# x and w_in converted to bf16 by the loads themselves: an induced-attention and PReLU feed-forward kernel on one core

## The chip, the core and the metric

The kernel runs on one core of a Trainium2 chip. The metric is the device time of one execution in microseconds. The engines are called as in the profile: PE (matrix products; PEld is its weight load), DVE, ACT and POOL (elementwise work), SP (here only an issuer of transfers). A name with q (SPq, POOLq) is the engine's instruction queue, which is worked through in order. 16 DMA engines carry the transfers that any queue issues.

## The reference

Four batches of 12,480 rows with 128 channels, 32 inducing rows, and a hidden layer of 2,048:

```
def mab(q, kv):
    s = scale * (q @ kv.transpose(0, 2, 1))
    s = s - s.max(-1, keepdims=True)
    a = np.exp(s)
    a /= a.sum(-1, keepdims=True) + 1e-09
    return a @ kv
h = mab(I, x)                      # 32 rows attend to all rows of a batch
y = mab(x, h).reshape(49920, 128)  # every row attends to those 32
t = y @ w_in
out = (np.maximum(t, 0.0) + alpha * np.minimum(t, 0.0)) @ w_out
```

All inputs and the output are f32 in memory.

## The kernel before

**Pieces.** Each batch of x is cut into six full pieces of 2,048 rows (1 MB, 16 tiles of 128 rows) and one of 192 rows (`xs_left`, `xn_left`). The order of work on them is the list `pieces`: the first full piece, the short one, then the other five. Within a full piece partition p holds 16 consecutive rows, so a load reads 8 KB in a row per partition.

**First stage, per batch.** `a_load` (L244) loads a piece as f32 into one of four `xs` buffers, from SP's queue. `a_cast` (L260) makes it bf16 (`xn`), on POOL (L272, L277), once on ACT (L270). It is then transposed to `xT`: by PE in the first batch (`a_turn_pe`, L286, copies on DVE L296 and ACT L294), by a transposing transfer from SP's queue in the others (`a_turn`, L281). `a_scores` (L310, L328, L337) gives the scores against the inducing rows with a running extremum, `a_exp` (L350) the exponentials, `a_fac` (L368, L375) the rescaling of earlier pieces, `a_e1` or `a_e1_pe` (L397, L398) a transpose of these, and `a_h` (L410, L423) adds the piece to h, for which it needs `xn` again. The end of the stage (`a_max`, `a_factors`, `a_den`, `a_sum`) gives `hT` (L478), and `a_w` (L486) the product `HW` of h with w_in (`w_in_b`, bf16).

**Second stage and main loop.** For each group of 2,048 rows DVE, ACT and POOL make the 32 softmax weights of each row (`b_scores` to `b_mul`; on POOL: L605, the sums L591 and L615, and L636), which a transposing transfer turns (`b_turn`, L645) into `a`. The main loop has 392 visits, four for each block of four tiles. A visit makes four products `hh` from `a` and `HW` (L692), applies a ReLU to them on ACT (L704) or DVE (L706), and the next visit multiplies these with `W1` (L717), which is w_out times one minus alpha. The rest of the PReLU is linear and enters through `Amat` (`linear`, L742). `finish` (L753) copies the sums (L768, L770) and SP stores them, from three `ob` buffers.

**What orders the work.** The first batch's first stage, the head, has nothing beside it: it is written out by hand as a string of steps, `order` (L911), where c is a cast, t a PE transpose, s scores, x exponentials, e their transpose, h the sum, w some products that keep PE busy. Ahead of it the first five pieces are loaded (L800); `load_next` (L851) issues the sixth and seventh, then w_in and w_out, as casts of earlier pieces free a buffer. `prepare_weights` (L901), behind step h3, casts w_in on POOL (L902), turns it (L903) and makes `W1` (L877) and `AW` (L886) on POOL. The first stage of the other batches is spread over the main loop: `at(n, ...)` puts a step behind visit n. A planner (`Plan`) gives each ReLU and copy to ACT or DVE from costs listed with these steps; loads, casts and POOL's steps carry no cost. In it the load of a piece stands three visits ahead of the number m of its piece, the cast six behind, the transpose eight behind, the scores fifteen behind. `tails` (L543) loads, casts and turns the short pieces of all batches for the last two blocks.

Of the kernel before, what the change touches and what calls it, by code (L numbers as in the profile page):

```python
# [22 lines left out]
P = 128  # L23
R = 4
ST = 16
# [6 lines left out]
def kernel(  # L32
# [9 lines left out]
    nc = tc.nc  # L42
    f32 = mybir.dt.float32
    bf16 = mybir.dt.bfloat16

    B, N, C = x.shape
# [25 lines left out]
    place = {s: p for p, s in enumerate(pieces)}  # L72

    const = ctx.enter_context(tc.tile_pool(name="const", bufs=1))
    xs_pool = ctx.enter_context(tc.tile_pool(name="xs", bufs=4))
    xn_pool = ctx.enter_context(tc.tile_pool(name="xn", bufs=sum(full)))
    xt_pool = ctx.enter_context(tc.tile_pool(name="xt", bufs=2))
    s1_pool = ctx.enter_context(tc.tile_pool(name="s1", bufs=3))
    e1_pool = ctx.enter_context(tc.tile_pool(name="e1", bufs=6))
# [147 lines left out]
    def new_state(b):  # L227
        st = State()
        st.b = b
        st.xT = xt_pool.tile([C, NT, P], bf16, name="xT", tag="xT")  # L230
        st.xn, st.xs, st.s1, st.e1T, st.e1 = {}, {}, {}, {}, {}
        st.e2, st.m2, st.den2, st.rc, st.rep = {}, {}, {}, {}, {}

        st.mx = sm_pool.tile([P, NS], f32, name="mx", tag="mx")
        st.rm = sm_pool.tile([P, NS], f32, name="rm", tag="rm")
        st.fac = sm_pool.tile([P, NS], f32, name="fac", tag="fac")
        st.da = sm_pool.tile([P, NS], f32, name="da", tag="da")
        st.den = sm_pool.tile([P, NS], f32, name="den", tag="den")
        st.hs = h_pool.tile([P, C], f32, name="hs", tag="hs")
        nc.gpsimd.memset(st.mx[:], HIGH)  # L240
        nc.gpsimd.memset(st.da[:], 0.0)
        return st

    def a_load(st, s):  # L244
        r0, nt, last = supers[s]
        if full[s]:
            st.xs[s] = xs_pool.tile([P, ST, C], f32, name="xs", tag="xs")
            nc.sync.dma_start(
                out=st.xs[s][:],
                in_=x[st.b, r0 : r0 + nt * P, :].rearrange("(p j) c -> p j c", p=P),  # L250
            )
        else:
            st.xs[s] = xs_left
            for t in range(nt):
                n = last if t == nt - 1 else P
                nc.sync.dma_start(
                    out=xs_left[:n, t, :], in_=x[st.b, r0 + t * P : r0 + t * P + n, :]
                )

    def a_cast(st, s, part=None, act=False):  # L260

        r0, nt, last = supers[s]
        xs = st.xs[s]
        if full[s]:
            if s not in st.xn:
                st.xn[s] = xn_pool.tile([P, ST, C], bf16, name="xn", tag="xn")
            h = ST // 2
            ts = slice(0, ST) if part is None else slice(part * h, part * h + h)
            if act:
                nc.scalar.copy(out=st.xn[s][:, ts], in_=xs[:, ts])  # L270
            else:
                nc.gpsimd.tensor_copy(out=st.xn[s][:, ts], in_=xs[:, ts])  # L272
        else:
            st.xn[s] = xn_left
            for t in range(nt):
                n = last if t == nt - 1 else P
                nc.gpsimd.tensor_copy(out=xn_left[:n, t, :], in_=xs[:n, t, :])  # L277

    def a_turn(st, s):
        nt = supers[s][1]  # L280
# [262 lines left out]
    def tails(part):  # L543

        if part == 0:
            nc.sync.dma_start(out=xb[:, :B, :], in_=whole(x))
            for i, w in enumerate(halves):
                nc.sync.dma_start(out=xb[w, B:, :], in_=half(x, i))
        elif part == 1:
            nc.gpsimd.tensor_copy(out=xbn[:], in_=xb[:])  # L550
        else:
            nc.sync.dma_start_transpose(out=xbT[:], in_=xbn[:].rearrange("p j c -> p (j c)"))

# [229 lines left out]
        plan.then(work)  # L783


    ident32 = const.tile([P, P], f32, name="ident32")
    make_identity(nc, ident32[:])
    st = new_state(0)
    ind_f = const.tile([M, C], f32, name="ind_f")
    nc.scalar.dma_start(out=ind_f[:], in_=inducing)  # L790
    al_f = const.tile([NK, P], f32, name="al_f")
# [1 line left out]
    alT = const.tile([P, NK], f32, name="alT")  # L793
    hTs = [const.tile([C, M], bf16, name=f"hT{b}") for b in range(B)]
    HWs = [const.tile([P, NV * P], bf16, name=f"HW{b}") for b in range(B)]
    xb = const.tile([P, NB, C], f32, name="xb")
    xbn = const.tile([P, NB, C], bf16, name="xbn")
    xbT = const.tile([C, NB, P], bf16, name="xbT")
    xs_left = const.tile([P, supers[-1][1], C], f32, name="xs_left")
    for s in pieces[:5]:  # L800
        a_load(st, s)
    xn_left = const.tile([P, supers[-1][1], C], bf16, name="xn_left")
    e1T_left = const.tile([P, supers[-1][1] * P], bf16, name="e1T_left")
    for t in (xn_left, e1T_left):
        nc.vector.memset(t[:], 0.0)
    ident = const.tile([P, P], bf16, name="ident")
    nc.vector.tensor_copy(out=ident[:], in_=ident32[:])

# [21 lines left out]
    AW = rep_pool.tile([P, NK, C], bf16, name="AW")  # L830
    winT = rep_pool.tile([P, NK, C], bf16, name="winT")
    W1 = const.tile([P, NK, C], bf16, name="W1")
    w_in_b = const.tile([C, DFF], bf16, name="w_in_b")
    Amat = const.tile([C, C], bf16, name="Amat")
    ind_b = const.tile([M, C], bf16, name="ind_b")
    nc.scalar.copy(out=ind_b[:], in_=ind_f[:])
# [9 lines left out]
    )  # L846

    a2s = {}
    w_in_f = w_out_f = None

    def load_next(p):  # L851

        nonlocal w_in_f, w_out_f
        if p + 5 < NS:
            a_load(st, pieces[p + 5])
        elif w_in_f is None:
            w_in_f = xs_pool.tile([C, DFF], f32, name="w_in_f", tag="xs")
            nc.sync.dma_start(out=w_in_f[:], in_=moe_w_in)
        elif w_out_f is None:
            w_out_f = xs_pool.tile([P, NK, C], f32, name="w_out_f", tag="xs")  # L860
            nc.sync.dma_start(out=w_out_f[:], in_=moe_w_out.rearrange("(k p) c -> p k c", p=P))

    def warm(n):

        ps = sums(1)
# [33 lines left out]
        nc.vector.tensor_copy(out=Amat[:], in_=ps[:])  # L899

    def prepare_weights():  # L901
        nc.gpsimd.tensor_copy(out=w_in_b[:], in_=w_in_f[:])  # L902
        nc.sync.dma_start_transpose(out=winT[:], in_=w_in_b[:])  # L903
        for i in range(NV):
            weights(i, nc.gpsimd)
        for i in range(NV):
            linear_weights(i)
# [1 line left out]


    order = """  # L911
        c00 t00 c01 t02 t01 c10 c21 c20 t10 s0 x0 t22 s1 c31 x1 t21 t20 c30 t32 t31 s2 f1 e0 c41
        t30 e1 x2 c40 c51 f2 c50 t42 s3 e2 t41 x3 f3 c60 t40 t51 t52 c61 h0 s4 t50 e3 t60 x4 t62
        t61 s5 f4 e4 s6 h1 h2 x5 h3 m0 h4 x6 e5 r0 e6 w1 f5 h5 w1 f6 h6 w2 d0 w1 g0 w2
    """
    assert NS == 7 and len(pieces) == 7 and not full[-1]
    cast = set()
    for step in order.split():
        f, p, part = step[0], int(step[1]), int(step[2:] or 0)
        s = pieces[p]  # L920
        if f == "c":
            a_cast(st, s, part, act=(p == NS - 1 and part == 1))
            cast.add((p, part))
            if p != 1 and (p, 1 - part) in cast:
                load_next(p - (p > 1))
        elif f == "t":
            a_turn_pe(st, s, part)
        elif f == "w":
            warm(p)
        elif f in "mrdg":  # L930
            {"m": a_max, "r": a_factors, "d": a_den, "g": a_sum}[f](st)
        else:
            {"s": a_scores, "x": a_exp, "f": a_fac, "e": a_e1_pe, "h": a_h}[f](st, s)
        if step == "h3":
            prepare_weights()
# [74 lines left out]
    for b, s, nt in groups[1:]:  # L1010
# [13 lines left out]
        at(when[5], on, b, b_rec, s, nt, cost=[("v", 160)])  # L1024
        at(when[6], on, b, b_mul, s, nt)
        at(when[7], on, b, b_turn, s, 0, nt)
    for part in range(3):
        at(first[B, 0] - 50 + 8 * part, tails, part)
    for b in range(B - 1):
        n = first[b, 0] - 1  # L1030
        if b:
            at(n - 4, lambda b=b: states.__setitem__(b + 1, new_state(b + 1)))
        for p, s in enumerate(pieces):
            m = n + (8 * (p - 1) if p > 1 else p)
            f = full[s]
            if b or p > 1:
                at(m - 3, on, b + 1, a_load, s)
            at(m + 6, on, b + 1, a_cast, s)
            at(m + 8, on, b + 1, a_turn, s)
            at(m + 15, on, b + 1, a_scores, s, cost=[("s", 310), ("v", 800 if f else 460)])  # L1040
            at(m + 16, on, b + 1, a_exp, s, cost=[("a", 717 if f else 430)])
            at(m + 18, on, b + 1, a_fac, s, cost=[("a", 450)] if p else [])
            at(m + 17, on, b + 1, a_e1, s)
            at(m + (24 if f else 26), on, b + 1, a_h, s, cost=[("s", 320), ("v", 260)])
        m = n + 8 * (NS - 2) + 15
        at(m + 2, on, b + 1, a_max, cost=[("a", 200)])
        at(m + 4, on, b + 1, a_factors, cost=[("s", 800), ("v", 70), ("a", 205)])
        at(m + 8, on, b + 1, a_den, cost=[("s", 500), ("v", 370)])
        at(m + 11, on, b + 1, a_sum, cost=[("s", 500), ("v", 110)])
        at(m + 12, on, b + 1, a_w, cost=[("s", 310)])  # L1050
        at(m + 12, on, b + 1, a_w_copy, cost=[("a", 487)])
        at(m + 15, on, b + 1, a_lin, cost=[("s", 160), ("v", 190)])
# [66 lines left out]
```

## Time and profile before

| | us |
|---|---|
| median of three runs | 602.05 (601.94 to 602.33) |
| profiled execution, first to last instruction (span) | 600.4 |
| median less span | 1.65 |
| PE, ACT, DVE, POOL busy in the span | 585.3, 552.9, 520.5, 218.3 |
| casts of x on POOL, 29 full or half pieces | 45.1 |
| cast of w_in on POOL | 1.89 |
| bytes moved | 80.51 MB, 134 GB/s on average |

The profile gives no time of the profiled execution beside its span; the runs' times are without a profile. PE, DVE, ACT and POOL in the profile are shares of busy time. The views that the prediction uses are: the slices, in which a digit is the busy share of a fortieth of the span in tenths; the chain that ended last, which goes back from the last instruction to what released each step; the timeline, whose rows are start, length, engine, line, operation and shapes, with the idle time ahead and its releaser in brackets; the busy time by stages; and the DMA view, which gives GB/s in fortieths of the stretch asked for.

### The profile page before, as it was taken

How to read it: one execution, taken by the hardware profiler on the slowest of the kernel's cores; microseconds unless marked ns; L12 is line 12 of the kernel's file. 1: busy time of each engine (PE TensorE's matmuls, PEld its weight loads, DVE VectorE, ACT ScalarE, POOL GpSimd, SP SyncE). 2: the span in 40 equal slices, each digit the busy share in tenths (PEclk: the TensorE clock that was granted, in tenths of full speed). 3: DMA queues.
4: the chain of work that ended last, by engine and by line, in shares of the span. 5: the costliest groups of instructions: out<-in, count | busy, mean ns of one | idle time of the engine just before them, and what ended most of it. 6: DMA issues, size and time to landing. Idle time of an engine off the chain costs nothing.

```text
span 600.4 us, 22604 instructions
## 1 busy us (share of the span) xinstructions
PE 585.3 (97%) x9405; PEld 438.4 (73%) x9407; DVE 520.5 (87%) x935; ACT 552.9 (92%) x1130; POOL 218.3 (36%) x253
## 2 busy tenths in 40 slices
PE   5899999999999999999999999999999999999997
PEld 3567777777777777777777777777777777777775
DVE  4678988988998998988898988988899899899895
ACT  3889999999999999999989999999999999999995
POOL 5655625313415526223236255134034034044110
PEclk9999999999999999999999999999999999999999
DMA  8859979333176999542256998841431331531321
GB/s 338 277 156 209 210 182 213 88 83 73 55 207 163 232 204 202 113 81 72 64 140 189 238 226 158 161 84 53 79 83 55 89 84 43 117 97 46 86 68 46
DMA packets 122198, 80.51 MB, mean 134 GB/s; under 512 B 103744, under 2 KB 106096, under 8 KB 118896
## 3 DMA queue, kind: packets, MB, share of 16 engines
q1 hardware_dynamic: 122016, 79.05, 54.0%
q8 instruction: 73, 1.20, 0.8%
q14 instruction: 29, 0.24, 0.1%
q10 hardware_dynamic: 80, 0.02, 0.0%
HBM read 28.07 MB, written 25.56 MB: 89 GB/s over the span
## 4 chain that ended last, share of the span: by engine, by line
PE 94%; ACT 2%; DMA 1%; DVE 1%; SPq 0%; issue 0%; POOL 0%; DVEq 0%; ACTq 0%
PE bp L717 65%; PE hh L692 22%; PE bp L742 2%; PE hh L525 2%; DMA xs<-in_x_dram 1%; PE hh L410 1%; PE hh L310 1%; ACT e1T L350 0%; ACT e L398 0%; ACT den L375 0%; ACT xT L294 0%; PE hh L486 0%; ACT fac L368 0%; ACT gt L704 0%; POOL xn L272 0%
## 5 line engine op out<-in xcount | busy, mean ns | idle before, releaser
L704 ACT ACTIVATE gt<-hh 128x512 bf16<-128x512 f32 (+1 forms) x904 | 474.5, 602 | 27.0 <-PE hh L692 18.6
L706 DVE TENSOR_SCALAR gt<-hh 128x512 bf16<-128x512 f32 (+1 forms) x664 | 428.7, 683 | 49.2 <-PE hh L692 39.4
L717 PE MATMUL bp<-W,gt 128*128 128x128 bf16 x6240 | 417.8, 220 | 0.0
L717 PEld LDWEIGHTS <-gt 128*128 128x128 bf16 x6240 | 349.4, 98 | 86.9 <-issue 79.7
L692 PE MATMUL hh<-a,HW 32*128 32x512 bf16 (+2 forms) x1664 | 159.9, 370 | 0.5 <-DVE e L558 0.3
L636 POOL TENSOR_TENSOR rep<-e,rc 128x2048 bf16<-128x2048 f32 (+1 forms) x24 | 84.5, 3519 | 16.1 <-DVE rc L628 16.1
L605 POOL TENSOR_TENSOR e<-e,smx 128x512 f32<-128x512 f32 (+1 forms) x24 | 24.6, 1025 | 180.5 <-DVE smx L600 180.5
L692 PEld LDWEIGHTS <-HW 32*128 32x128 bf16 x1664 | 41.1, 91 | 42.2 <-issue 5.8
L591 POOL TENSOR_TENSOR t<-e 128x256 f32<-128x256 f32 (+1 forms) x24 | 17.2, 718 | 135.8 <-ACT e L567 135.8
L272 POOL CAST xn<-xs 128x2048 bf16<-128x2048 f32 (+1 forms) x29 | 45.1, 1566 | 8.6 <-DMA xs<-in_x_dram 8.0
L768 ACT COPY ob<-bp 128x512 f32<-128x512 f32 (+1 forms) x53 | 31.1, 587 | 1.5 <-PE bp L717 0.6
L591 POOL TENSOR_TENSOR t<-t 128x128 f32<-128x128 f32 (+3 forms) x96 | 29.1, 303 | 7.5
L770 DVE COPY ob<-bp 128x512 f32<-128x512 f32 x41 | 28.0, 683 | 0.4
L328 DVE TENSOR_SCALAR_CACHE_REDUCE s<-hh 128x512 f32<-128x512 f32 (+1 forms) x28 | 17.9, 640 | 6.1 <-PE hh L310 5.9
L742 PE MATMUL bp<-HA,a 32*128 32x128 bf16 (+1 forms) x392 | 20.0, 214 | 0.0
L742 PEld LDWEIGHTS <-a 32*128 32x128 bf16 (+1 forms) x392 | 15.3, 93 | 6.1 <-issue 0.5
L350 ACT ACTIVATE e1T<-s,rm 128x512 bf16<-128x512 f32 x24 | 17.3, 723 | 2.0 <-DVE rm L337 2.0
L600 DVE TENSOR_REDUCE smx<-e 128x16 f32<-128x512 f32 (+1 forms) x24 | 15.9, 662 | 0.0
L567 ACT ACTIVATE e<-e 128x512 f32<-128x512 f32 (+1 forms) x24 | 14.8, 615 | 0.0
L525 PE MATMUL hh<-hT,xT 128*128 128x32 bf16 x384 | 13.5, 176 | 0.2
L525 PEld LDWEIGHTS <-xT 128*128 128x128 bf16 x384 | 12.3, 96 | 1.1 <-issue 0.8
L423 DVE SCALAR_TENSOR_TENSOR hs<-hs,fac,hh 128x128 f32<-128x128 f32 (+1 forms) x24 | 8.2, 341 | 4.2 <-PE hh L410 2.5
(99 smaller groups left out, 185.4 us busy)
## 6 DMA issues: line engine op xcount, KB each, us to landing
out_dram<-ob SPq DMA_DIRECT2D x97, 256.0 KB, 2.4
xs<-in_x_dram SPq DMA_DIRECT2D x24, 1024.0 KB, 6.2
w_in_f<-in_moe_w_in_dram SPq DMA_DIRECT2D x1, 1024.0 KB, 9.1
a<-rep SPq DMA_TRANSPOSE x25, 4.6
xT<-xn SPq DMA_TRANSPOSE x18, 6.1
e<-e1T SPq DMA_TRANSPOSE x18, 3.4
xs_left<-in_x_dram SPq DMA_DIRECT2D x4, 64.0 KB, 5.2
xb<-in_x_dram SPq DMA_DIRECT2D x1, 256.0 KB, 3.7
```

The lines of the kernel that those rows point to most:

```text
L272: nc.gpsimd.tensor_copy(out=st.xn[s][:, ts], in_=xs[:, ts])
L525: nc.tensor.matmul(ps[w, t, :], st.xT[:, tile0[s] + t, w], hTs[b][:], start=True, stop=True)
L591: nc.gpsimd.tensor_tensor(out=t[:, :n], in0=src[:, :n, :w], in1=src[:, :n, w : 2 * w], op=ADD)
L605: nc.gpsimd.tensor_tensor(out=st.e2[s][:, :n], in0=st.e2[s][:, :n], in1=st.m2[s][:, :n].unsqueeze(2).broadcast_to([P, n, M]), op=SUB,)
L636: nc.gpsimd.tensor_tensor(out=rep[:, :n], in0=st.e2[s][:, :n].unsqueeze(2).broadcast_to([P, n, R, M]), in1=rc[:, :n].unsqueeze(2).unsqueez ...
L692: nc.tensor.matmul(hh[:, w], HWs[b][rows, i * P : (i + 1) * P], a2[rows, t0 : t0 + nt, :].rearrange("m j t -> m (j t)")[:, w], start=True, ...
L704: nc.scalar.activation(out=gt[:, :cols], in_=hh[:, :cols], func=RELU)
L706: nc.vector.tensor_relu(gt[:, :cols], hh[:, :cols])
L717: nc.tensor.matmul(blk.acc[:, t * C : (t + 1) * C], gt[:, t * P : (t + 1) * P], W1[:, k, :], start=(not blk.begun), stop=(k == NK - 1), sk ...
L742: nc.tensor.matmul(blk.acc[w, t * C : (t + 1) * C], blk.a2[rows, blk.t0 + t, w], HAs[b][rows, :], start=(not blk.begun and t == 0), stop=F ...
L768: nc.scalar.copy(out=ob[:, :nt], in_=acc)
L770: nc.vector.tensor_copy(out=ob[:, :nt], in_=acc)
```

## The change

x is loaded straight into bf16 buffers by transfers whose destination has another type than their source, issued from POOL's queue. `xs`, `xs_left`, `a_cast` and `load_next` go. `xn` has nine buffers instead of six. In the head all pieces, then w_in (into `w_in_b`, converted) and w_out (f32, into a buffer of its own in `rep_pool`), are issued from POOL one behind the other. Two memsets of `new_state` and the first two pieces stand ahead of `make_identity`, which is on POOL too; the other pieces and the weights stand behind it. In the main loop a piece's load stands two visits ahead of m instead of three. `tails` loads straight into `xbn`.

```
     def a_load(st, s):
         r0, nt, last = supers[s]
         if full[s]:
-            st.xs[s] = xs_pool.tile([P, ST, C], f32, name="xs", tag="xs")
-            nc.sync.dma_start(
-                out=st.xs[s][:],
+            st.xn[s] = xn_pool.tile([P, ST, C], bf16, name="xn", tag="xn")
+            nc.gpsimd.dma_start(
+                out=st.xn[s][:],
                 in_=x[st.b, r0 : r0 + nt * P, :].rearrange("(p j) c -> p j c", p=P),
             )
         else:
...
+                nc.gpsimd.dma_start(
+                    out=xn_left[:n, t, :], in_=x[st.b, r0 + t * P : r0 + t * P + n, :]
+                )
...
         if part == 0:
-            nc.sync.dma_start(out=xb[:, :B, :], in_=whole(x))
+            nc.gpsimd.dma_start(out=xbn[:, :B, :], in_=whole(x))
             for i, w in enumerate(halves):
-                nc.sync.dma_start(out=xb[w, B:, :], in_=half(x, i))
-        elif part == 1:
-            nc.gpsimd.tensor_copy(out=xbn[:], in_=xb[:])
+                nc.gpsimd.dma_start(out=xbn[w, B:, :], in_=half(x, i))
...
+    xn_left = const.tile([P, supers[-1][1], C], bf16, name="xn_left")
+    e1T_left = const.tile([P, supers[-1][1] * P], bf16, name="e1T_left")
+    for t in (xn_left, e1T_left):
+        nc.vector.memset(t[:], 0.0)
+    st = new_state(0)
+    for s in pieces[:2]:
+        a_load(st, s)
     ident32 = const.tile([P, P], f32, name="ident32")
     make_identity(nc, ident32[:])
-    st = new_state(0)
...
-    for s in pieces[:5]:
+    for s in pieces[2:]:
         a_load(st, s)
...
+    w_in_b = const.tile([C, DFF], bf16, name="w_in_b")
+    nc.gpsimd.dma_start(out=w_in_b[:], in_=moe_w_in)
+    w_out_f = rep_pool.tile([P, NK, C], f32, name="w_out_f")
+    nc.gpsimd.dma_start(out=w_out_f[:], in_=moe_w_out.rearrange("(k p) c -> p k c", p=P))
...
     def prepare_weights():
-        nc.gpsimd.tensor_copy(out=w_in_b[:], in_=w_in_f[:])
         nc.sync.dma_start_transpose(out=winT[:], in_=w_in_b[:])
...
-                at(m - 3, on, b + 1, a_load, s)
-            at(m + 6, on, b + 1, a_cast, s)
+                at(m - 2, on, b + 1, a_load, s)
```

The steps c00 to c61 of `order` go; the rest of the string stays as it was.

More of the change, by code (lines that the diff above doesn't have):

```diff
@@ L74 @@
     const = ctx.enter_context(tc.tile_pool(name="const", bufs=1))
-    xs_pool = ctx.enter_context(tc.tile_pool(name="xs", bufs=4))
-    xn_pool = ctx.enter_context(tc.tile_pool(name="xn", bufs=sum(full)))
+    xn_pool = ctx.enter_context(tc.tile_pool(name="xn", bufs=sum(full) + 3))
     xt_pool = ctx.enter_context(tc.tile_pool(name="xt", bufs=2))
@@ L230, in new_state @@
         st.xT = xt_pool.tile([C, NT, P], bf16, name="xT", tag="xT")
-        st.xn, st.xs, st.s1, st.e1T, st.e1 = {}, {}, {}, {}, {}
+        st.xn, st.s1, st.e1T, st.e1 = {}, {}, {}, {}
         st.e2, st.m2, st.den2, st.rc, st.rep = {}, {}, {}, {}, {}
@@ L246, in a_load @@
         if full[s]:
-            st.xs[s] = xs_pool.tile([P, ST, C], f32, name="xs", tag="xs")
-            nc.sync.dma_start(
-                out=st.xs[s][:],
+            st.xn[s] = xn_pool.tile([P, ST, C], bf16, name="xn", tag="xn")
+            nc.gpsimd.dma_start(
+                out=st.xn[s][:],
                 in_=x[st.b, r0 : r0 + nt * P, :].rearrange("(p j) c -> p j c", p=P),
             )
[L252 to L272, printed above, removed]
         else:
@@ L276, in a_cast @@
                 n = last if t == nt - 1 else P
-                nc.gpsimd.tensor_copy(out=xn_left[:n, t, :], in_=xs[:n, t, :])
+                nc.gpsimd.dma_start(
+                    out=xn_left[:n, t, :], in_=x[st.b, r0 + t * P : r0 + t * P + n, :]
+                )
     def a_turn(st, s):
@@ L795 @@
     HWs = [const.tile([P, NV * P], bf16, name=f"HW{b}") for b in range(B)]
-    xb = const.tile([P, NB, C], f32, name="xb")
     xbn = const.tile([P, NB, C], bf16, name="xbn")
     xbT = const.tile([C, NB, P], bf16, name="xbT")
-    xs_left = const.tile([P, supers[-1][1], C], f32, name="xs_left")
-    for s in pieces[:5]:
+    for s in pieces[2:]:
         a_load(st, s)
[L802 to L805, printed above, removed]
+    w_in_b = const.tile([C, DFF], bf16, name="w_in_b")
+    nc.gpsimd.dma_start(out=w_in_b[:], in_=moe_w_in)
+    w_out_f = rep_pool.tile([P, NK, C], f32, name="w_out_f")
+    nc.gpsimd.dma_start(out=w_out_f[:], in_=moe_w_out.rearrange("(k p) c -> p k c", p=P))
     ident = const.tile([P, P], bf16, name="ident")
@@ L832 @@
     W1 = const.tile([P, NK, C], bf16, name="W1")
-    w_in_b = const.tile([C, DFF], bf16, name="w_in_b")
     Amat = const.tile([C, C], bf16, name="Amat")
@@ L848 @@
     a2s = {}
[L849 to L861, printed above, removed]
     def warm(n):
@@ L911 @@
     order = """
-        c00 t00 c01 t02 t01 c10 c21 c20 t10 s0 x0 t22 s1 c31 x1 t21 t20 c30 t32 t31 s2 f1 e0 c41
-        t30 e1 x2 c40 c51 f2 c50 t42 s3 e2 t41 x3 f3 c60 t40 t51 t52 c61 h0 s4 t50 e3 t60 x4 t62
-        t61 s5 f4 e4 s6 h1 h2 x5 h3 m0 h4 x6 e5 r0 e6 w1 f5 h5 w1 f6 h6 w2 d0 w1 g0 w2
+        t00 t02 t01 t10 s0 x0 t22 s1 x1 t21 t20 t32 t31 s2 f1 e0 t30 e1 x2 f2 t42 s3 e2 t41 x3 f3
+        t40 t51 t52 h0 s4 t50 e3 t60 x4 t62 t61 s5 f4 e4 s6 h1 h2 x5 h3 m0 h4 x6 e5 r0 e6 w1 f5 h5
+        w1 f6 h6 w2 d0 w1 g0 w2
     """
     assert NS == 7 and len(pieces) == 7 and not full[-1]
-    cast = set()
     for step in order.split():
@@ L920 @@
         s = pieces[p]
[L921 to L926, printed above, removed]
+        if f == "t":
             a_turn_pe(st, s, part)
@@ L1026 @@
         at(when[7], on, b, b_turn, s, 0, nt)
-    for part in range(3):
-        at(first[B, 0] - 50 + 8 * part, tails, part)
+    for part in range(2):
+        at(first[B, 0] - 50 + 16 * part, tails, part)
     for b in range(B - 1):
```

## The prediction

> **What bounds the kernel now.** I read the page first: the busy slices, then the shares of the chain that ended last.
>
> ```profile
> PE   5899999999999999999999999999999999999997
> ...
> DMA  8859979333176999542256998841431331531321
> ...
> PE 94%; ACT 2%; DMA 1%; DVE 1%; SPq 0%; issue 0%; POOL 0%; DVEq 0%; ACTq 0%
> ```
>
> One slice is 15 us. PE is full from the third slice to the last but one; only the first two (the first 33 us) and the end are not. The busy time by stages says the same: each row gives the stage, its length, then busy us and instructions of PE, PEld, DVE, ACT and POOL, the clock, the DMA share and GB/s.
>
> ```profile
> 12.00:20.00 8.00, 6.44 (x97) 4.56 (x95) 6.11 (x18) 7.77 (x22) 6.60 (x7) 1.00 1.02 425
> 20.00:26.00 6.00, 4.83 (x107) 3.51 (x108) 4.62 (x15) 5.77 (x16) 2.24 (x2) 1.00 0.72 221
> 33.00:100.00 67.00, 66.88 (x1062) 49.20 (x1061) 58.65 (x110) 64.48 (x136) 33.48 (x36) 1.00 0.86 192
> 100.00:300.00 200.00, 200.00 (x3230) 150.04 (x3228) 178.18 (x317) 191.15 (x391) 69.36 (x81) 1.00 0.54 126
> ```
>
> From 33 us on PE has no idle time (the waits there list one PE wait of 0.3 us). POOL's and ACT's casts of x in that stage stand beside PE's work, so what they cost is already hidden. Only the head can give time back. There the DMA engines are full from 6 to 20 us, at 425 GB/s. The chain of waits for 0 to 36 us (start, length, what) names what binds:
>
> ```profile
> 2.92 8.86 DMA xs<-in_x_dram
> 11.78 0.05 issue
> 11.83 1.05 POOL xn L272
> 12.88 0.05 issue
> 12.92 0.52 PE hh L291 x4
> ...
> 19.46 0.94 ACT xn L270
> ...
> 32.85 1.14 PE hh L692 x4
> ```
>
> A load of x, then one cast of half a piece (1.05 us) on POOL, then a long chain on ACT with the other cast (0.94 us) inside it. The timeline around the last piece shows what waited:
>
> ```profile
> 19.30 1.04 POOL L272 CAST xn<-xs 128x1024 bf16<-128x1024 f32 x1 [0.47 <-DMA xs<-in_x_dram]
> 20.40 1.07 PE L291 MATMUL hh<-ident,xn 128*128 128x128 bf16 x16 [0.55 <-POOL xn L272]
> 21.06 1.02 DVE L296 COPY xT<-hh 128x1024 bf16<-128x1024 bf16 x2 [0.34 <-PE hh L291]
> ```
>
> POOL waits for the transfer, PE for POOL, DVE for PE: the last piece is late at every step, by its transfer. Casts begin at 9.36, 11.83, 14.32, 16.81 and 19.30 us: 2.49 us a piece of 1.049 MB, 421 GB/s.
>
> **The change, part by part.**
>
> *Casts gone, head.* Eleven half-casts on POOL and one on ACT. Because the transfers set the pace, only the cast behind the last landing is on the path: 20.40 - 19.25 = 1.15 us less the 0.1 us of signalling that any landing needs, so 1.05 us. ACT's 0.94 us comes on top only if ACT is what is late then; after the last piece's transposes DVE runs without a gap from 21.06 to 23.6 us (two xT copies 1.02, two score reductions 1.37, the maxima), and ACT's exp of that piece starts behind it at 23.97. So I count ACT's cast at nothing here; if DVE were not the later of the two it would be worth up to 0.94.
>
> *Loads move from SP's queue to POOL's.* SP issued the first load at 0.74 us. POOL comes past its constants at 0.73 and now has two memsets (0.04 apart) ahead of the load: 0.85. The issue itself has no row on POOL. Its lower bound is SP's shortest x load, 0.33 us; the first one took 0.41. The upper one is an SP issue of a transfer with many short rows, 1.88 us (the transpose winT). Nothing shows a gain, since the first load cannot start before the engine does. I take 0.83 us, SP's issue of w_out's 2,048 rows, the nearest row in which a list is long. Then data flows later by (0.85 - 0.74) + (0.83 - 0.41) = 0.5 us; at the bounds by 0.0 and 1.6. All further issues (0.83 each) are shorter than a piece's 2.49 us and hide behind the data. The identity now stands behind three issues on POOL: 0.85 + 3 x 0.83 + 0.57 = 3.9 us instead of 1.3; at 1.88 each, 7.1. PE's first user waits until 4.83 for ind_b anyway, and x's first transposes ran at 7.39, so this costs nothing at either end.
>
> *Rate of a transfer that also converts.* No row shows one. It reads the same 1.049 MB in 8 KB rows and writes half. Lower end: the plain load, 2.49 us a piece. Upper end: the transposing transfers, which also rearrange data on the way. The DMA view of 45.5 to 53 us shows them alone on full engines:
>
> ```profile
> GB/s 0 0 0 0 0 0 0 27 208 217 218 210 208 213 218 221 218 216 205 194 215 220 132 5 1 0 76 371 360 426 394 284 240 229 306 215 214 202 203 217
> ```
>
> That is 215 GB/s, 4.9 us a piece. Below nothing: if the written bytes were the limit, a piece could take 1.25 us. I take 2.49, because the transposes move packets under 512 B (3,090 of 3,346 in that view), and the converting load keeps the plain load's long rows. The Trainium skill, "DMA: Bandwidth & Descriptors", section "Bandwidth", speaks against it: its table of GpSimd-issued loads has 16 MB in 79.0 us, which is an estimated 4.9 us per piece, while the GB/s column beside it (425) says half of that. By the first the sum would be that of rival 1 below, by the second the forecast; the trace of before has no load from GpSimd to decide it.
>
> *w_in, w_out.* w_in's cast (23.03 to 24.92 on POOL) goes; its next users are the winT transpose, used at 40.9, and HW's product at 29.06. Hidden now, nothing gained. w_out is still f32 and lands behind x and w_in as before (about 26); the four products for W1 begin at 26.39 and PE needs the first slice at 33.9, 6.5 us after it is done (27.43).
>
> *The main loop.* POOL loses 18 casts of 1.89 us and gains 18 issues of 0.4 to 1.9: nothing to PE. A load now stands behind POOL's sums (ending 65.99 in the trace, where SP issued at 64.08, so 1.9 us later) and its transpose is due ten visits on, some 14 us. Landing takes a median 6.2 us, so some 6 us remain; with 4.9 us a piece, 3.5. If that cover went, the transpose would hold SP's queue, the outputs behind it, and PE once the three ob buffers are full. Batch 1's first two loads fall behind POOL's weight products, from 27 to 34.5 us; the transpose at 45.77 leaves 5 us. The planner's costs never held casts or loads, so its choices stay. tails: three loads and no cast, 21 us ahead of their transpose: nothing.
>
> **Sum.** -1.05 + 0.5 = -0.55 us, in the head; at the issue's bounds -1.05 and +0.55. The span is 600.4 us and the runs' median 602.05; the 1.65 us around it stay. Forecast 602.05 - 0.55 = 601.5 (span 599.85), own range 601.0 to 602.6. A measurement of this kernel tells about 0.2% (1.2 us) from no change, so this counts as within it.
>
> **Rivals.**
>
> 1. *The converting transfer is slow.* x of one batch is 6.39 MB: 15.0 us at 425 GB/s. At 215 it is 29.7, so the last piece lands 14.7 later; less 0.55, and less some 1 us of DVE's backlog that is gone by then: +13, 615. At some 290 GB/s, which the busy time by stages shows while w_out's 512 B rows flow (22 to 23 us: 295), 22.0: +7 - 0.55 = +6.5, 608.5. It makes the kernel slower past the bound as soon as 6.39 MB takes 1.75 us longer than 15.0, so under 380 GB/s. For it: the transposes show that a transfer that rearranges data can run at half. Against it: long rows. Chances 0.27 for 215 or worse, 0.18 for in between.
> 2. *The writes were the limit.* Then pieces come faster than ACT can take them; ACT, 97% busy from 12 to 20 us, becomes the bound, its 0.94 us counts, and its first exp (11.61 us) starts some 1.5 us earlier: 602.05 - 2.4 = 599.6. With ACT's 0.94 counting alone: 600.5. Against it: 425 GB/s read and written alike leaves open which side is full. Chance 0.14.
> 3. *POOL writes w_out's list row by row.* Nine issues at 0.83 end near 9 us; the data (2.6), landing (2) and one product (1.04) must fit ahead of 33.3, so a list of over some 19 us, 9 ns a row, is late, and 25 us would cost 6: 608. SP's 0.83 us speaks against it. Chance 0.07.
>
> The forecast has 0.34.
>
> **How the numbers follow.** Faster by over 0.2%: rival 2, 0.14. Within: the forecast, 0.34. Slower: 0.27 + 0.18 + 0.07 = 0.52. The single likeliest case is still the forecast, since the slower ones spread over 603 to 615 and beyond. The range, 600.3 to 616, leaves out the fast half of rival 2 (0.07) and rates under 210 GB/s (0.1).
>
> **What would show it.** Right: x's landings 2.5 us apart, the first one near 6.8 us, the last piece's transposes near 19.85 instead of 20.40, the first L692 row of the solid part near 32.3, and PE without idle time behind it. Rival 1: DMA share full but GB/s low from 6 us on, and PE waiting for x's transfers. Rival 2: ACT without gaps from 9 us on. Rival 3: W1's first product later than 32 us. Wrong altogether: PE waits for xT, a or ob in the main loop.

## The result and the profile after

The changed kernel is slower: a median of 634.25 us over four executions (624.09 to 635.91) against 602.09 us (601.94 to 602.33). The ratio is 1.0439, 95% interval 1.0407 to 1.0471; it leaves out the two executions above 635 us, which showed the lowest granted clocks. The profiled execution took 632.92 us, with a span of 631.1 us.

The page of the changed kernel: busy slices of PE, the granted clock, the DMA share, and the shares of the chain that ended last.

```profile
PE   5898969999999999999999897989999999999997
...
PEclk9998989999999999999999898989999999999999
DMA  8979799532256797741267989953313312532331
...
PE 80%; DMA 15%; ACT 1%; issue 1%; DVE 1%; POOL 1%; SPq 0%; DVEq 0%; ACTq 0%; POOLq 0%
PE bp L697 56%; PE hh L672 19%; DMA a<-rep 13%; DMA xn<-in_x_dram 2%; PE bp L722 2%; PE hh L507 1%; PE hh L392 1%; PE hh L292 1%; POOL xn L249 0%; ACT gt L684 0%; DVE gt L686 0%; PE hh L468 0%; DVE ob L750 0%; ACT den L357 0%; PE hh L446 0%
```

PE has holes in the slices from 47 to 95 us and again from 347 to 426 us, the granted clock dips with them, and a transfer that the kernel before had nowhere on its chain, the transpose `a<-rep`, now holds 13% of it. (L672 and L697 here are L692 and L717 of before.) The chain from 0 to 60 us shows both halves of the story:

```profile
5.78 13.65 DMA xn<-in_x_dram
19.43 0.05 issue
19.48 0.86 PE hh L273 x12
...
31.93 1.15 PE hh L672 x4
...
48.14 11.09 DMA a<-rep
```

The head is shorter: the main loop's first solid products begin at 31.93 us instead of 32.85. Then, at 48 us, PE is held up by a transpose that takes 11.09 us; in the kernel before, none of the 25 took over 6.3. PE's waits from 33 us on (us in total, times, longest):

```profile
PE hh L672 <- DMA a<-rep: 13.3, 8, 2.9
PE hh L292 <- DMA xT<-xn: 8.2, 4, 4.3
PE bp L697 <- issue: 2.0, 1, 2.0
PE hh L300 <- DMA xT<-xn_left: 0.4, 1, 0.4
```

That makes 24 us in which PE stood still; before, the same list has one wait of 0.3 us, for DVE. (For the 2.0 us in the third row, a hole at 110 us, the profile names no releaser.) Most of the rest of the 30.7 us between the spans is the clock: PE's busy time grew from 585.3 to 592.3 us for the same products, 7 us, at a mean granted clock of 0.985 instead of 1.000. The busy time by stages shows where (columns as in the prediction):

```profile
60.00:100.00 40.00, 34.69 (x522) 25.61 (x520) 29.51 (x55) 31.84 (x68) 10.15 (x17) 0.92 0.82 122
100.00:300.00 200.00, 195.00 (x3167) 146.35 (x3163) 173.58 (x312) 186.64 (x384) 63.12 (x76) 1.00 0.60 115
300.00:400.00 100.00, 91.78 (x1423) 69.02 (x1419) 80.17 (x141) 85.59 (x174) 31.71 (x42) 0.97 0.75 119
400.00:620.00 220.00, 217.34 (x3497) 165.62 (x3494) 194.81 (x321) 202.99 (x400) 59.99 (x75) 0.99 0.37 79
```

The clock fell to 0.92 in the stage with the longest hole (4.3 us, at 83 us); the stage from 100 to 300 us lost 5.0 us in holes of up to 2.0 and kept 1.00. What is lost from 400 us on is lost before 414 us, by transposes that the last load of the loop, issued at 395 us, still met. From 420 us on PE is full.

What happens at 48 us is plain in the timeline of POOL and SP of the changed kernel:

```profile
44.51 3.61 POOL L616 TENSOR_TENSOR rep<-e,rc 128x2048 bf16<-128x2048 f32 x1 [0.99 <-PE bp L697]
48.06 0.59 POOL L249 DMA_DIRECT2D xn<-in_x_dram  x1
48.14 9.08 SPq L625 DMA_TRANSPOSE a<-rep  x1
```

POOL's product L616 makes `rep`. Behind it, in POOL's queue, stands a load of x; in SP's queue stands the transpose that waits for `rep`. Both start at once. In the kernel before both were in SP's queue, one behind the other:

```profile
50.59 2.43 SPq L645 DMA_TRANSPOSE a<-rep  x1
53.07 0.75 SPq L248 DMA_DIRECT2D xs<-in_x_dram  x1
```

So was their data. The DMA view of the kernel before for 50 to 55 us, in steps of 0.125 us, has two output stores, then the transpose at some 215 GB/s; the load's data follows after its end:

```profile
DMA  0000899999999998989999999999999999000100
GB/s 1 0 0 0 328 344 377 360 442 344 377 295 229 246 229 262 350 168 215 211 199 201 215 215 221 209 215 227 229 342 205 180 57 4 0 0 2 8 8 10
```

Running at once, here, they do more than share the engines: they stall. The DMA view of the changed kernel for 47 to 52 us, in the same steps:

```profile
DMA  8399599999990900002000101010010009019689
GB/s 172 72 315 170 113 375 70 211 141 2 106 35 0 2 0 0 0 0 33 0 0 0 33 0 33 0 33 0 0 33 0 2 18 537 16 23 393 187 270 351
```

For some 2.5 us from 48.4 on next to nothing moves, with two loads, two transposes and two output stores outstanding. It had begun before: a load issued at 42.94 us and the transpose of the short piece, issued at 43.12, are among them and land at 52.3 and 52.5. In the kernel before that transpose took 2.7 us.

### The profile page after: what moved, and what is told of

The parts are those of the page before. It is cut to its first block, busy times and chain, and to the rows that moved or that the text cites. A ratio compares the mean times of both kernels' runs of the same rounds, so it can differ in the third digit from the quotient of the medians.

```text
span 631.1 us, 22555 instructions
## 1 busy us (share of the span) xinstructions
PE 592.3 (94%) x9407; PEld 444.3 (70%) x9407; DVE 521.7 (83%) x935; ACT 554.4 (88%) x1129; POOL 190.7 (30%) x251
## 4 chain that ended last, share of the span: by engine, by line
PE 80%; DMA 15%; ACT 1%; issue 1%; DVE 1%; POOL 1%; SPq 0%; DVEq 0%; ACTq 0%; POOLq 0%
PE bp L697 56%; PE hh L672 19%; DMA a<-rep 13%; DMA xn<-in_x_dram 2%; PE bp L722 2%; PE hh L507 1%; PE hh L392 1%; PE hh L292 1%; POOL xn L249 0%; ACT gt L684 0%; DVE gt L686 0%; PE hh L468 0%; DVE ob L750 0%; ACT den L357 0%; PE hh L446 0%
## 5 line engine op out<-in xcount | busy, mean ns | idle before, releaser
L697 PE MATMUL bp<-W,gt 128*128 128x128 bf16 x6240 | 423.1, 221 | 2.1 <-issue 2.0
L697 PEld LDWEIGHTS <-gt 128*128 128x128 bf16 x6240 | 354.3, 99 | 89.4 <-issue 82.5
L672 PE MATMUL hh<-a,HW 32*128 32x512 bf16 (+2 forms) x1664 | 160.6, 374 | 13.9 <-DMA a<-rep 13.3
L616 POOL TENSOR_TENSOR rep<-e,rc 128x2048 bf16<-128x2048 f32 (+1 forms) x24 | 84.5, 3521 | 21.2 <-DVE rc L608 20.1
L672 PEld LDWEIGHTS <-HW 32*128 32x128 bf16 x1664 | 42.1, 91 | 56.2 <-issue 20.2
L292 PE MATMUL hh<-xT,IT 128*32 128x512 bf16 x96 | 10.4, 406 | 8.2 <-DMA xT<-xn 8.2
L249 POOL DMA_DIRECT2D xn<-in_x_dram x24 | 14.0, 589 | 1.6 <-issue 1.0
L507 PEld LDWEIGHTS <-xT 128*128 128x128 bf16 x384 | 12.3, 96 | 1.1 <-issue 0.8
```

Source lines behind the costliest of these rows:

```text
L507: nc.tensor.matmul(ps[w, t, :], st.xT[:, tile0[s] + t, w], hTs[b][:], start=True, stop=True)
L616: nc.gpsimd.tensor_tensor(out=rep[:, :n], in0=st.e2[s][:, :n].unsqueeze(2).broadcast_to([P, n, R, M]), in1=rc[:, :n].unsqueeze(2).unsqueez ...
L672: nc.tensor.matmul(hh[:, w], HWs[b][rows, i * P : (i + 1) * P], a2[rows, t0 : t0 + nt, :].rearrange("m j t -> m (j t)")[:, w], start=True, ...
L697: nc.tensor.matmul(blk.acc[:, t * C : (t + 1) * C], gt[:, t * P : (t + 1) * P], W1[:, k, :], start=(not blk.begun), stop=(k == NK - 1), sk ...
```

## The experiments

**Theories.** 1, overlap: a load that comes through another queue than SP's and runs beside SP's transposing transfers stalls both; before, SP's queue kept them in a row. 2, conversion: only a converting transfer does that. 3, GpSimd (the engine that the profile calls POOL): its way of issuing does it. Below, "beside a load" means that the load of a full piece and a transpose, each taken from issue to landing, overlap by over 1 us; the times are medians from issue to landing in the trace.

**r1, r2: which half.** r1 has the changed head and the old loop, r2 the old head and the changed loop.

```
 r1, loop                                  r2, loop
 at(m - 3, on, b + 1, a_load, s)  # SP     at(m - 2, on, b + 1, a_load_cast, s)  # POOL
 at(m + 6, on, b + 1, a_cast, s)
```

> The head of the changed kernel (converting loads of batch 0, w_in and w_out from POOL's queue), the main loop of the kernel before (f32 loads from SP's queue, casts on POOL). Both theories say that the converting loads are harmless where no transposing transfer runs beside them: the solid part of L692's products begins 0.9 us earlier (32.85 before, 31.93 in the changed kernel), PE has no idle time behind it, so 602.1 - 0.9 = 601.2 us, 600.8 to 601.6. If the damage came from the head (a late weight, a buffer), it would be 620 or more.

> The head of the kernel before, the loop of the changed one (converting loads from POOL's queue; eight xn buffers instead of nine for want of room). Both theories say that all of the loss is here: 625 to 637 us, a<-rep landing about 10 us where a load of x is in flight, granted clock under 0.99. If the loss needs the changed head, it would be near 602.

r1: 602.15 us against 602.22, ratio 0.9999 (0.9990 to 1.0007). r2: 629.03 us, ratio 1.0449 (1.0433 to 1.0465). All of the loss is in the loop, as expected. The head's gain is not: in r1's trace the first L717 product is 0.3 us ahead of before, not 0.9, and the span ends level, with a granted clock of 0.96 in the last 20 us where before it was 1.00. The changed head is worth nothing that can be measured.

**r3, r4: conversion or queue.** The kernel before, with the loop's f32 loads issued from another queue (in r3 one visit later, as in the changed kernel):

```
-                at(m - 3, on, b + 1, a_load, s)
+                at(m - 2, on, b + 1, a_load, s, nc.gpsimd)   # r3
+                at(m - 3, on, b + 1, a_load, s, nc.scalar)   # r4
```

> The kernel before, but the loop's loads of x (still f32, still cast on POOL) are issued from POOL's queue, at the visits at which the changed kernel issues them. Theory 1, two rings: any load that comes through another queue than SP's stops SP's transposing transfers while it runs, converting or not; then 615 to 637 us, a<-rep landing 9 to 12 us beside a load. Theory 2, conversion: only a converting transfer stalls beside transposing ones; then 602 to 604 us and a<-rep landing 5 to 6 us.

> The kernel before, but the loop's loads of x (f32, cast on POOL) are issued from ACT's queue at their old visits, so neither GpSimd nor a conversion is involved. Theory 1, two rings: 612 to 637 us, transposes beside a load land 9 to 12 us after issue. Theory 2, conversion, and a third one, that a list written by GpSimd is what disturbs: 602 to 606 us (21 issues on ACT, of some 0.5 us each, partly hidden), transposes landing as before (a<-rep 4.6, xT 6.1 us).

r3: 646.56 us, ratio 1.0726 (1.0696 to 1.0757), slower still without any conversion. PE waits for the same transposes:

```profile
PE hh L692 <- DMA a<-rep: 32.5, 9, 5.4
```

Beside a load `a<-rep` takes 9.4 us, without one 4.6, so theory 2 falls. Why r3 is some 12 us slower than the changed kernel was not followed up. r4: 609.0 us, ratio 1.0107 (1.0092 to 1.0123), between what theories 1 and 3 expected, and little of it is PE's wait for a transpose:

```profile
PE hh L692 <- DMA a<-rep: 1.7, 1, 1.7
```

In r4 ACT issues its loads at their own visits, some 3 us away from `a<-rep`, and few run beside it (six, 5.7 us; the worst took 8.4). It had left out the coincidence, so it told nothing between 1 and 3.

**r11: ACT's queue, at the moment of a<-rep.** r4 with pieces 0, 3 and 5 two visits earlier.

```
-                at(m - 3, on, b + 1, a_load, s, nc.scalar)
+                at(m - (3 if p and p % 2 == 0 or p == 1 else 5), on, b + 1, a_load, s, nc.scalar)
```

> The run with f32 loads from ACT's queue, with the loads of pieces 0, 3 and 5 moved two visits ahead, to the visit at which SP issues a<-rep, so that load and transpose run together as in the changed kernel, but with no GpSimd list and no conversion. If any second queue beside a transposing one is enough: a<-rep beside a load lands in 8 to 11 us and the time is 612 to 640 us. If it is GpSimd's queue in particular: a<-rep lands in 5 to 6.5 us and the time is 606 to 611 us, as without the move.

623.06 us, ratio 1.0345 (1.0324 to 1.0367): two visits' difference costs 14 us. In r11's timeline

```profile
78.27 1.76 SPq L645 DMA_TRANSPOSE a<-rep  x1
78.45 0.34 ACTq L248 DMA_DIRECT2D xs<-in_x_dram  x1
```

start together; this transpose lands 12.4 us after its issue and the load 9.7. Beside a load `a<-rep` takes 9.3 us (eight), without one 4.7 (seventeen), and PE's waits are back:

```profile
PE hh L692 <- DMA a<-rep: 14.4, 6, 3.7
```

Neither GpSimd nor conversion is needed, so theory 3 falls too. How close the two start matters: r4's five `a<-rep` whose load was issued 2 us or more behind them landed in 4.6 to 6.0 us; r11's eight, with the load issued between 1.4 us ahead and 0.8 us behind, took 6.9 to 12.4.

Is this only two transfers sharing the engines? In part it may be. In r11's view of 79 to 87 us the engines do not stand still as they did in the changed kernel at 48 us; they move 211 GB/s on average (steps of 0.2 us):

```profile
DMA  9999999999992325516353771969939689098799
GB/s 381 369 451 349 238 243 173 206 236 268 219 131 83 127 84 127 127 44 252 127 212 127 294 255 32 448 195 205 284 110 376 76 316 372 3 351 178 76 237 68
```

But a plain load needs 2.5 us of the engines, so a transpose of 4.7 us that merely gave way to it would land within 7.2, an estimate from these two numbers; seven of r11's eight took 8.6 us or more. How much is sharing and how much is loss was not separated.

The Trainium skill, "DMA: Bandwidth & Descriptors", section "Rules for kernel authors", says that a transpose next to ordinary DMAs needs nothing done for it; the row is about transposes that corrupt each other's data. For the data that may hold; for the time the runs disagree: 4.7 against 9.3 us here, 4.6 against 9.7 in the changed kernel.

**r7, r9: move the loads off that moment.** Loads of pieces 0, 3 and 5 in front of the product L616 instead of behind it; r7 is the changed kernel with that move, r9 is r3 with it.

```
-                at(m - 2, on, b + 1, a_load, s)
+                at(m - (2 if p and p % 2 == 0 or p == 1 else 9), on, b + 1, a_load, s)
```

> The changed kernel, but the loads that stood two visits ahead of m behind the product L616 on POOL (pieces 0, 3 and 5 of a batch) stand nine visits ahead of m, and so in front of that product, as the other pieces' loads do already. Theory 1a, coincidence: a load that POOL issues right behind the product starts with the transpose a<-rep, which waits for the same product, and the two share the engines; moved ahead, a<-rep has the engines to itself: a<-rep lands in 5 to 7 us, PE's waits for it fall from 13.3 us to under 4, 604 to 613 us. Theory 1b, any overlap: transposes are in flight most of the time, and xT and e1T, which SP works through ahead of a<-rep, hold it up as before: 620 to 637 us.

> The third run (plain f32 loads from POOL's queue, casts on POOL) with the same move as the first of this call: loads of pieces 0, 3 and 5 nine visits ahead of m. Theory 1a, coincidence: PE's waits for a<-rep fall from 32.5 us to under 8 and the time from 646 to 606 to 615 us; what this run has over the converting one is what conversion itself is worth. Theory 1b, any overlap: 630 us or more.

r7: 617.82 us, ratio 1.0262 (1.0229 to 1.0296). Half of the loss goes, between the two expectations: `a<-rep` lands in 7.1 us beside a load (five of them), but two loads now start with an `xT` transpose, which takes 11.9 us beside a load, and SP's queue holds `a<-rep` behind it. PE's wait:

```profile
PE hh L672 <- DMA a<-rep: 8.6, 5, 2.8
```

r9: 643.38 us, ratio 1.0630 (1.0600 to 1.0659), hardly better than r3, and not as theory 1a had it: PE's wait for `a<-rep` fell, but that for `xT<-xn`, which r3 did not have, took its place (the traced execution, 650.3 us, was the longest of six):

```profile
PE hh L310 <- DMA xT<-xn: 29.7, 5, 10.0
PE hh L692 <- DMA a<-rep: 6.7, 4, 2.4
```

There the load stands behind a cast on POOL that an `xT` transpose waits for; at 45.7 us the two start within 0.1 us, and the transpose lands 19.5 us later. So it is not the one coincidence with `a<-rep`: an `xT` transpose that starts with a load fares no better.

**r8: short rows.** The loop's converting loads in four parts, 1 KB written per row.

```
-            nc.gpsimd.dma_start(out=st.xn[s][:], in_=xv)
+            step = ST if st.b == 0 else BT
+            for j in range(0, ST, step):
+                nc.gpsimd.dma_start(out=st.xn[s][:, j : j + step], in_=xv[:, j : j + step])
```

> The changed kernel, but each of the loop's converting loads is cut into four, with 2 KB read and 1 KB written per partition instead of 8 and 4 (four issues on POOL, some 2.3 us instead of 0.6). If the two queues take turns packet by packet, a transposing packet (18 ns) waits for a load's packet of about 80 ns instead of 324, and the transposes beside a load land in 5 to 7 us instead of 9.7: 604 to 615 us. If it is something else that stops both (a stall of the engines, as the packets of over 3 us suggest), short rows do not help: 622 us or more.

634.44 us, ratio 1.0518 (1.0494 to 1.0542); `a<-rep` beside a load takes 8.9 us, and PE waits for it longer than in the changed kernel (13.3):

```profile
PE hh L672 <- DMA a<-rep: 21.0, 8, 5.2
```

The load's packets did get short (98 ns in the middle instead of 324), and it helped nothing. That the two queues merely take turns, packet by packet, with the long packets first in line, is not the explanation.

**r10, r13: loads in the gaps.** The changed kernel with all its converting loads, but one full piece per 16 visits, put behind the first addition of `b_tree` on POOL; in the trace these loads start 1.6 to 8.4 us ahead of SP's next transpose. Batch 1's first four pieces are loaded in the head.

```
-    def b_tree(src, n):
+    def b_tree(src, n, loads=()):
...
             src, w = t, w // 2
+            while loads:
+                a_load(*loads.pop(0))
```

> The changed kernel with all its converting loads, but in the loop one per 16 visits instead of two, issued behind the first addition of L571 on POOL (which waits for ACT's exp, some 4 us ahead of SP's next transpose); batch 1's first four pieces are loaded in the head, behind w_out. Theory 1, overlap of POOL's loads with SP's transposes: nearly all overlap is gone, a<-rep lands in 4.6 to 7 us, PE waits under 2 us for transfers in the loop, 601 to 604 us. A theory by which converting loads from POOL cost the loop something of their own (the lists, SBUF, the clock): over 610 us.

Three of six executions took 602.06 to 602.46 us, the other three 615.1 to 622.0. The traced one was of the first kind, the time that theory 1 expected. Its busy time by stages:

```profile
33.00:100.00 67.00, 66.88 (x1070) 49.46 (x1068) 58.19 (x109) 64.47 (x136) 23.67 (x31) 1.00 0.80 147
100.00:300.00 200.00, 200.00 (x3226) 149.91 (x3226) 178.08 (x316) 191.02 (x391) 64.95 (x86) 1.00 0.58 115
300.00:580.00 280.00, 280.00 (x4482) 211.45 (x4480) 251.96 (x427) 264.03 (x527) 85.84 (x105) 1.00 0.47 96
```

PE is full in every stage and the clock is 1.00, with the converting loads still there. One `a<-rep` met the end of a load and landed in 5.6 us; the longest of all took 7.2. Eight `xT` transposes still ran beside a load, each issued 1.6 to 3.4 us behind it; they took 7.7 us instead of 5.4, and PE waited for none. So an overlap cost nothing where the transpose had slack. For the executions of 615 us and over the same kernel was traced once more:

> The same kernel as the run with loads in the gaps, once more, for a trace of one of its slow executions (615 to 622 us) if one comes: by theory 1 it has transposes beside loads that the fast one has not, and PE waits for a<-rep or winT. A fast one (602 us) would leave that open.

It took 619.04 us, and PE's longest wait is one that the traced r10 did not have:

```profile
PE hh L867 <- DMA winT<-w_in_b: 13.6, 1, 13.6
```

The transpose `winT`, issued at 22.93 us beside batch 1's loads (22.92 to 25.07), landed 31.8 us later; in the traced r10, issued beside the same loads, 14.3. The two loads took 24.0 and 25.6 us. Between 38 and 48 us the engines moved this, in steps of 0.25 us:

```profile
DMA  9990994995993991189994995999998919999939
GB/s 25 27 44 17 57 41 62 70 55 53 45 71 38 76 60 36 36 78 65 76 62 87 83 124 71 69 102 109 55 67 61 85 35 63 83 83 48 65 36 83
```

The engines count as busy and move 63 GB/s, less than the transposes alone (215 in the prediction's view) or loads alone (425).

**r12: winT alone.** r10, with batch 1's loads moved behind the products for W1 (pieces 0 and 1) and into the first gaps.

```
             weights(i, nc.gpsimd)
+        for q in pieces[:2]:
+            a_load(1, q)
```

> The run with loads in the gaps took 602.1 to 602.5 us in half of its executions and 615 to 622 in the others. In its trace the transpose winT, issued at 22.8 us beside batch 1's first loads, lands 14.4 us later, at 37.2, and PE needs it at 40. Here those loads move: pieces 0 and 1 between the products W1 and AW on POOL (some 30 us), 2 and 3 to the first gap, 4 and 5 to the second, 6 to the third. If a late winT makes the slow executions: all within 601 to 604 us. If they come from somewhere in the loop: still 615 to 622 in some.

Twelve executions of 602.30 to 605.99 us, median 603.18, ratio 1.0018 (1.0006 to 1.0029). `winT` lands in 6.9 us, and the long executions are gone. Not quite as expected: three executions exceed 604, and one of PE's waits in the loop is left:

```profile
PE hh L674 <- DMA a<-rep: 0.7, 1, 0.7
```

No version beats the kernel before.

## Why the prediction was wrong

- **Head: right in kind, of no use.** The rate of a converting transfer was taken from the plain load, 2.49 us a piece. Measured: pieces land at 9.57, 12.05, 14.53, 16.97 and 19.43 us, 2.47 apart. The first landed at 6.52 us (said: near 6.8). The Trainium skill, "DMA: Bandwidth & Descriptors", section "Bandwidth", has two columns for loads issued from GpSimd; the head, whose loads also convert, agrees with the GB/s column and not with the 79.0 us for 16 MB. POOL's issue took 0.55 us and 0.77 for the first, w_out's list 1.20 (assumed: 0.83 each; rival 3 is out, the weights' product began at 26.23, before at 26.39). The first issue started at 1.29 us, not 0.85. Signalling between a landing and the next step took 0.05 us (11.78 to 11.83 in the prediction's own chain), not 0.1, so the cast was worth 1.10. The last piece's transposes ran at 19.48 (said: 19.85), the loop's first solid products at 31.93 (said: 32.3). So the sum of -0.55 was -0.92 in this trace, and -0.3 in r1's, where it did not reach the time; why the two differ is not known.
- **Rivals 1 and 2: out.** Neither the rate fell nor did the writes set it.
- **The failed step: "The main loop."** It reads: "POOL loses 18 casts of 1.89 us and gains 18 issues of 0.4 to 1.9: nothing to PE." It counted the slack of the load itself (some 6 us) and was right about that: PE never waits for `xn` in the loop. It took the landing time of 6.2 us, and silently that of all transposes, as properties of the transfers. They were properties of SP's queue, which had kept the loads and the transposes in a row. With the loads in a second queue (changed kernel against kernel before, both beside a load) `a<-rep` beside one takes 9.7 us instead of 5.2, `xT<-xn` 12.3 instead of 6.7, and `e<-e1T` 8.9 instead of 2.3. The term was sized at 0 and measured 24 us of PE's waits and 7 us of clock.
- **What was at hand to see it.** The prediction itself noted that the load now stands behind POOL's instructions, but asked only whether it would be late. For pieces 0, 3 and 5 it stands behind L616, which `a<-rep` waits for, so the two had to start together. And in the trace of before transposes are in flight for 79% of the time from 45 to 117 us; a load placed outside that queue without regard to them was likely to meet one.
- **The sign of failure was named**: "PE waits for xT, a or ob in the main loop" is what the profile shows, but no rival gave it a mechanism or a price.

**What stays open.** Why two queues stall each other so is not settled. Turn-taking in which a transpose waits for long packets is out (r8). Packets of 4 KB that last up to 3.6 us and stretches with next to no bytes show that the engines wait; for what, no run shows. Why the same kernel had `winT` land after 14.3 us in one execution and after 31.8 in another is open too. That only a transposing transfer suffers is not shown: output stores beside a load also took twice as long (4.7 us in r10 against 2.3 without), and no run had a load and a store alone. Nor was it tried to hold a load back until a transpose has landed.

## What to carry to other kernels

Transfers in one queue have an order that no line of the code states; before moving one of them to another queue, list what it will run beside, above all transposing transfers, and what waits for those. A move also ties the transfer to its new queue's neighbours: here the load came to stand right behind the instruction that released the transpose. Where a load must leave the queue, put it where the trace shows no transpose in flight that something waits for: the converting loads cost some 30 us in one place and 0.8 us in another (r12).

## What the runs showed of the hardware

- A transposing transfer that runs beside a load from another queue and starts close to it takes about twice as long (`a<-rep` 9.3 us instead of 4.7, plain f32 load from ACT's queue in r11), at the worst more than four times: `winT` 31.8 us instead of 6.9 (r13 against r12). The load suffers too: in the changed kernel's loop 7.6 us, in r10 without a transpose 5.5.
- A load from POOL's queue that converts f32 to bf16 reads at the rate of a plain one, 1.049 MB in 2.47 us, when nothing transposes beside it.
- Waits on PE can be paid twice: the granted clock fell to 0.92 in the stage with the longest hole, and over the whole span this made 7 us on top of 24; the stage from 100 to 300 us, with holes of up to 2.0 us, kept 1.00.
